# Attention with a soft mixture of experts on one core: value products split three to one, and the late softmax sums moved to GpSimd

## The chip, the cores and the metric

One NeuronCore of a Trainium2 chip. The metric is the device time of one execution in microseconds (us). Five engines matter: TensorE (PE, with its weight loads PEld), VectorE (DVE), ScalarE (ACT), GpSimd (POOL) and SyncE (SP), which issues most DMAs. Each engine executes its own list of instructions strictly in order, and waits on semaphores for the others.

## What is computed

```python
kv_flat = kv.reshape(B, H//4, 4, W//4, 4, C).mean(axis=(2, 4)).reshape(B, -1, C) @ w_sr
s = scale * (q @ kv_flat.transpose(0, 2, 1))          # 12288 queries x 768 keys, 4 batches
a = exp(s - s.max(-1)); a /= a.sum(-1) + 1e-09
x = (a @ kv_flat).reshape(B * N, C)                   # 49152 tokens x 128
logits = x @ phi                                      # 32 slots (8 experts x 4)
d = exp(logits - logits.max(0)); d /= d.sum(0) + 1e-09
slot_out = per expert: relu((d.T @ x) @ w1) @ w2      # 32 x 128
c = exp(logits - logits.max(1)); c /= c.sum(1) + 1e-09
out = c @ slot_out                                    # 49152 x 128
```

The last three lines of logits work are the "output softmax": over the 32 slots of each token. Its result can be multiplied with `slot_out` only when all tokens have been seen, so the output is written at the end.

## The kernel before

The queries are worked in 96 blocks of 512 (`NB`), 24 per batch. A group is 4 blocks (2048 tokens); there are 25 groups, since the last four blocks are split into one of three and one of one. A Python class `Plan` is a list scheduler: the kernel states each step with an engine, a cost, a due time and its dependences, and the class emits one fixed order of instructions per engine. The chip sees only these orders.

**A block.** PE makes the scores in 18 matmuls (L560 to L562, three PSUM tiles of two banks, `s`). DVE takes their maxima over keys (L578, L588, L590), PE brings these across partitions by the one rowmax matmul L598, and DVE finishes with L603 and the transpose L608, then subtracts the maximum from the scores (L616, four pieces), which frees the score tiles for the next block. ACT takes exponentials (L624, L628), and POOL forms the low half of their split to 16 bits (`plo`, L633).

**Value products.** For each of the 4 tiles of 128 queries of an earlier block, PE multiplies the exponentials with the values: 12 matmuls with the high half (L650, L651: "hi") and 6 with the low half (L658: "lo"). They accumulate in two PSUM banks that the plan hands out, `m_119` and `m_120`: tiles 0 and 1 in one (322 columns), tiles 2 and 3 in the other. The rowmax matmul L598 writes its 64 columns at the end of one of the same two banks, and so do the small products of a group (among them L778 and L834). ACT evacuates each pair of tiles (L668, 128x322).

**A group.** DVE, POOL and ACT turn 16 evacuated tiles into logits, and update running maxima and sums of the slots. For the output softmax of the group DVE takes the maxima over 32 slots (`k_max`, L852, one instruction per block), POOL subtracts them (`k_sub`, L857), ACT takes the exponential (L862), DVE sums (`k_sum`, L869, two per group), ACT adds 1e-09 (`k_add`, L874), DVE takes the reciprocal (`k_rec`, L879) and POOL multiplies (`k_mul`, L884). `k_add` and `k_rec` are joint over several groups: `JOIN = (0, 4, 12, 22)` gives spans of groups 0 to 3, 4 to 11 and 12 to 21. The products of groups 0 to 3 lie in the loop, all others behind it.

**Behind the loop (the tail).** The experts run (L1322 to L1384), their result is scaled and split (`shi`, L1390, on ACT; `slo` on DVE), and 25 chunks of output follow: PE transposes the softmax of a chunk (L1412), ACT and DVE split it (`chi`, L1418; `clo`, L1422), PE multiplies with `shi` and `slo` (L1434), ACT and DVE evacuate one half each (`o`, L1448, L1450; the first chunk in pieces, L1456 and L1458), and SP issues its write, 1.05 MB for a full chunk.

Of the kernel before, what the change touches and what calls it, by code (L numbers as in the profile page):

```python
# [36 lines left out]
class Plan:  # L37
# [22 lines left out]
    def emit(self):  # L60
# [31 lines left out]
        def bank(key):  # L92
            found = []
            for b in range(len(banks)):
                if key[0] == "pq":
                    t = gone(banks[b])
                    beside = banks[b] is not None and banks[b][1][0] == "px" and t == inf
                    if beside:
                        t = summed.get(banks[b], inf)
                    found.append((max(t, gone(tops[b])), not beside, b))  # L100
                else:
                    found.append((max(gone(banks[b]), gone(tops[b])), False, b))
            return min(found)
# [104 lines left out]
def attention_then_soft_moe(ctx: ExitStack, tc: tile.TileContext, qT, kv0, kvT, w_sr, w_srT, phi, w1, w2, outT):  # L208
# [130 lines left out]
    SPAN = 2  # L339
    KPS = 2  # L340
    KSD = 2
    KDUE = 4.0
    EARLY = FAST - 1
    AHEAD = 4
    JOIN = (0, AHEAD, 12, EARLY)
    KV0 = 14.5
# [283 lines left out]
    def plo(i, h):  # L630
# [3 lines left out]
        PP[i, h] += (lo,)  # L634

    def av_tile(i, k):
        if k % 2 == 0 and i == NB - 1:
            PX[i, k // 2] = ps.tile([P, 2, BQ], F32, tag=f"s{k // 2}", name=f"px_{i}_{k}")[:, :, :VW]
        elif k % 2 == 0:
            px = mt([P, 512], f"px_{i}_{k}")  # L640
            PX[i, k // 2] = px[:, : 2 * VW].rearrange("p (n c) -> p n c", n=2)
        return PX[i, k // 2][:, k % 2, :]

    def av_hi(i, k, t0):
        _, vhi, vlo = VU[i // BPB]
        px = PX[i, k // 2][:, k % 2, :] if t0 else av_tile(i, k)
        ks = slice(k * P, (k + 1) * P)
        for t in range(t0, t0 + AVS):
            p = PP[i, t // TH][0][:, t % TH, ks]
            nc.tensor.matmul(px, p, vhi[:, t, :], start=(t == 0 and (i >= AHD or k % 2 == 0)), stop=False)  # L650
            nc.tensor.matmul(px[:, 1:], p, vlo[:, t, :], start=False, stop=False)  # L651

    def av_lo(i, k):
        vhi = VU[i // BPB][1]
        px = PX[i, k // 2][:, k % 2, :]
        ks = slice(k * P, (k + 1) * P)
        for t in range(NT):
            nc.tensor.matmul(px, PP[i, t // TH][1][:, t % TH, ks], vhi[:, t, :], start=False, stop=(t == NT - 1 and (i >= AHD or k % 2 == 1)))  # L658

    def av_evac(i, k):  # L660
        g = GOF[i]
        if i == GB[g][0] and k == 0:
            XL[g] = gp.tile([P, TG, VW], F32, tag="xl", name=f"xl_{g}", bufs=2)
        o = (i - GB[g][0]) * TB + 2 * k
        if i == NB - 2 and k == 0:
            nc.vector.tensor_copy(XL[g][:, o : o + 2, :], PX.pop((i, k)))
        else:
            nc.scalar.activation(XL[g][:, o : o + 2, :], PX[i, k], AF.Copy)  # L668

# [178 lines left out]
    def k_max(g, u=None):  # L848
        o, n = GB[g][0] * TB, nt(g)
        if u is not None:  # L850
            o, n = o + u * TB, TB
        nc.vector.tensor_reduce(out=RM[:, o : o + n], in_=LL[:, o : o + n, :], axis=X, op=ALU.max)  # L852
# [56 lines left out]
    def dve(n):  # L909
        return n / 960 + 0.07  # L910
# [208 lines left out]
    def av_rest(i, k, m, p, prev):  # L1119
        los = [ops["lo", i, 0], ops["lo", i, 1]]  # L1120
        a2 = end_lo = op("PE", 6 * 0.072, 0.17, p + 0.8, prev + los, lambda: av_lo(i, k), use=[("plo", (i, 0)), ("plo", (i, 1)), m])
        if k % 2:
            g = GOF[i]
            first = i == GB[g][0] and k == 1
            x = ("xl", g)
            if i == NB - 1:
                v = k // 2
                q = HEAD + (i - 2) * PER + 0.01 * v
                a2 = op("DVE", 0.16, 0.08, q, [a2], lambda: l_x(v), use=[m], raw=0.05)
                a2 = op("DVE", 0.16, 0.08, q, [a2], lambda: l_r(v), raw=0.05)  # L1130
                a2 = ops["l", v] = op("DVE", 0.24, 0.08, q, [a2], lambda: l_l(v), use=[m], raw=0.05)
            ops["x", i, k // 2] = op(
                "DVE" if i == NB - 2 and k == 1 else "ACT", act(2 * VW) + (0.1 if i == NB - 2 and k == 1 else -0.03), 0.1, p - 2, [a2] + evs[-1:], lambda: av_evac(i, k // 2),
                acq=[x] if first else [], use=[m] + ([] if first else [x]),
            )
            evs.append(ops["x", i, k // 2])
        return [end_lo]
# [4 lines left out]
    def av_ops(i):  # L1142
# [6 lines left out]
        end = i == NB - 1  # L1149
        px = [(f"s{k // 2}" if end else "m", ("px", i, k // 2)) for k in range(TB)]  # L1150
        base = prev
        for k in range(TB if i < AHD else 0):
            m = px[k]
            p = T0 + AVD * PER + 1.3 * k
            if k == TB // 2:
                low = prev
                prev = base + [ops["r3", i + 1]]
            for t in range(0, NT, AVS):
                prev = [op("PE", 2 * AVS * 0.0702, 0.17, p, prev, lambda i=i, k=k, t=t: av_hi(i, k, t), acq=[m] if k % 2 == t == 0 else [], use=pp + ([m] if k % 2 or t else []))]
            if k % 2:  # L1160
# [98 lines left out]
    def k_first(g, a):  # L1259
# [3 lines left out]
        ops["ke", g] = op("ACT", act(n), 0.1, p, [a], lambda: k_exp(g))  # L1263

    for g in range(len(GB)):
        n = nt(g) * NS
        p = HEAD + (GB[g][0] + GB[g][1] + KLAG) * PER
        late = [] if g < FAST - 1 else end_ + [last[LG, "g"]]
        if late:
            a = [op("DVE", dve(n), 0.08, p, [ops["L", g]] + late, lambda g=g: k_max(g))] if g < FAST else []  # L1270
        else:
            a = [op("DVE", dve(TB * NS) + 0.05, 0.08, p, [ops["L", g]], lambda g=g, u=u: k_max(g, u), fill=p + 3 * PER) for u in range(GB[g][1])]
        if g < FAST:
            k_first(g, a)
        if g < EARLY:
            ops["ks", g] = [
# [337 lines left out]
```

## Time and profile before

| | |
|---|---|
| median of 3 runs | 1062.12 us (1062.01 to 1062.18) |
| the profiled execution | 1062.19 us |
| its span (first to last instruction) | 1060.4 us |
| busy PE / DVE / POOL / ACT | 1027.6 / 971.5 / 872.5 / 793.6 us |
| granted TensorE clock, mean | 0.996 |
| output written | 25.17 MB |

The span is 1.8 us shorter than the execution's own time, a constant that lies around it. The loop runs to about 965 us, the experts to about 995 us, and the output to the end. Busy shares are means over these three stages, which have different limits.

### The profile page before, as it was taken

The numbers are of one execution on the slowest core, as the hardware profiler recorded it, in microseconds if no ns is written. First come the engines' busy times: TensorE is split into PE (matmuls) and PEld (weight loads), VectorE is DVE, ScalarE is ACT, GpSimd is POOL, SyncE is SP. The second block draws the span as 40 slices with busy tenths as digits, with TensorE's granted clock in tenths as the row PEclk, the third lists the DMA queues.
The fourth block names the chain that finished last, engine by engine and source line by source line (L and its number), as shares of the span: only waits on it lengthen the run. The fifth ranks groups of instructions, "written<-read, shape, count | busy, mean of one in ns | idle before, by whom it ended". The sixth has DMA issues, their size and how long they took to land.

```text
span 1060.4 us, 24836 instructions
## 1 busy us (share of the span) xinstructions
PE 1027.6 (97%) x10261; PEld 880.3 (83%) x10261; DVE 971.5 (92%) x1552; ACT 793.6 (75%) x1046; POOL 872.5 (82%) x509
## 2 busy tenths in 40 slices
PE   8999999999999999999999999999999999999994
PEld 5788888888888888888888888888888888888452
DVE  6989999999999999999999999999999999998774
ACT  3777887888777787788787787788787787776463
POOL 0789998889989988889989988889988999895800
PEclk9999999999999999999999999999999999999998
DMA  9234510120137320120146310120110110112598
GB/s 370 112 83 89 119 54 3 42 87 15 41 72 148 71 56 2 41 100 2 41 87 134 86 41 1 41 100 1 41 41 2 42 41 1 41 41 91 198 416 368
DMA packets 15729, 89.17 MB, mean 84 GB/s; under 512 B 1664, under 2 KB 1920, under 8 KB 9344
## 3 DMA queue, kind: packets, MB, share of 16 engines
q1 hardware_dynamic: 11728, 69.47, 17.8%
q0 software_dynamic: 3312, 17.70, 8.9%
q8 instruction: 81, 1.33, 0.5%
q10 hardware_dynamic: 576, 0.41, 0.1%
q14 instruction: 32, 0.26, 0.1%
HBM read 58.87 MB, written 25.17 MB: 79 GB/s over the span
## 4 chain that ended last, share of the span: by engine, by line
PE 86%; DVE 7%; DMA 3%; ACT 1%; issue 1%; POOL 0%; SPq 0%; DVEq 0%; ACTq 0%; POOLq 0%
PE m L650 15%; PE m L658 14%; PE m L651 14%; PE s L560 12%; PE s L562 12%; PE s L561 11%; DMA outT<-o 2%; PE m L834 2%; DVE r L578 2%; DVE t L616 2%; PE po L1434 1%; DMA kv<-kv 1%; PE m L1406 1%; DVE m L603 1%; PE m L465 1%
## 5 line engine op out<-in xcount | busy, mean ns | idle before, releaser
L633 POOL TENSOR_TENSOR plo<-t,phi 128x1536 f16<-128x1536 f32 x190 | 599.0, 3163 | 92.9 <-ACT t L628 84.0
L624 ACT ACTIVATE phi<-t 128x1536 f16<-128x1536 f32 x192 | 283.5, 1478 | 148.0 <-DVE t L616 148.0
L578 DVE TRANSPOSE_TENSOR_REDUCE r<-s 128x32 f32<-128x1024 f32 x289 | 354.0, 1234 | 8.4 <-PE s L562 1.6
L650 PE MATMUL m<-vhi,phi 128*128 128x161 f16 x2280 | 353.2, 234 | 8.2 <-DVE m L603 7.3
L651 PE MATMUL m<-vlo,phi 128*128 128x160 f16 x2280 | 352.4, 233 | 0.0
L616 DVE TENSOR_TENSOR t<-s,mb 128x1024 f32<-128x1024 f32 (+1 forms) x384 | 342.0, 950 | 6.2
L628 ACT ACTIVATE t<-t 128x1536 f32<-128x1536 f32 x192 | 283.1, 1476 | 1.2
L650 PEld LDWEIGHTS <-phi 128*128 128x128 f16 x2304 | 224.1, 98 | 21.7 <-issue 21.3
L560 PE MATMUL s<-qhi,khi 128*128 128x512 f32 x574 | 237.0, 413 | 0.6 <-DVE t L616 0.4
L651 PEld LDWEIGHTS <-phi 128*128 128x128 f16 x2304 | 225.1, 98 | 12.1 <-issue 10.6
L562 PE MATMUL s<-qhi,klo 128*128 128x512 f32 x574 | 224.6, 391 | 0.0
L561 PE MATMUL s<-qlo,khi 128*128 128x512 f32 x574 | 223.9, 390 | 0.0
L658 PE MATMUL m<-vhi,plo 128*128 128x161 f16 x2280 | 223.5, 234 | 0.0
L658 PEld LDWEIGHTS <-plo 128*128 128x128 f16 x2304 | 171.9, 98 | 2.8 <-issue 2.7
L550 POOL TENSOR_TENSOR qlo<-q,qhi 128x512 fp32r<-128x512 f32 x95 | 127.5, 1342 | 23.9 <-ACT qhi L545 23.9
L562 PEld LDWEIGHTS s<-qhi,klo 128*128 128x128 f32 x574 | 107.7, 188 | 23.7
L560 PEld LDWEIGHTS s<-qhi,khi 128*128 128x128 f32 x574 | 107.9, 188 | 21.7 <-issue 2.6
L561 PEld LDWEIGHTS s<-qlo,khi 128*128 128x128 f32 x574 | 108.2, 189 | 19.4 <-issue 0.7
L668 ACT ACTIVATE xl<-m 128x322 f32<-128x322 f32 x189 | 81.3, 430 | 50.4 <-PE m L658 44.1
L608 DVE STREAM_TRANSPOSE mb<-m 128x512 f32<-128x512 f32 x96 | 68.3, 712 | 3.3
L545 ACT ACTIVATE qhi<-q 128x512 fp32r<-128x512 f32 x96 | 59.5, 620 | 2.8 <-DMA q<-qT 2.7
L603 DVE TENSOR_REDUCE m<-m 128x16 f32<-128x64 f32 x96 | 21.5, 224 | 22.6 <-PE m L598 19.2
(196 smaller groups left out, 840.4 us busy)
## 6 DMA issues: line engine op xcount, KB each, us to landing
q<-qT SPq DMA_DIRECT2D x23, 1024.0 KB, 4.9
outT<-o SPq DMA_DIRECT2D x22, 1024.0 KB, 8.3
kva<-kvT POOLq DMA_DIRECT2D x9, 1536.0 KB, 11.6
kva<-kvT SPq DMA_DIRECT2D x3, 1536.0 KB, 12.8
kv<-kv SPq DMA_DIRECT2D x6, 512.0 KB, 6.2
w<-w SPq DMA_DIRECT2D x2, 1536.0 KB, 6.3
w<-w SPq DMA_DIRECT2D x4, 768.0 KB, 4.1
kva<-kva POOLq DMA_DIRECT2D x3, 768.0 KB, 10.8
```

The lines of the kernel that those rows point to most:

```text
L550: eng.tensor_tensor(out=lo, in0=q_src(i), in1=hi.bitcast(F32), op=ALU.subtract)
L560: nc.tensor.matmul(s, khi[:, ks], hi, start=True, stop=False)
L561: nc.tensor.matmul(s, khi[:, ks], lo, start=False, stop=False)
L562: nc.tensor.matmul(s, klo[:, ks], hi, start=False, stop=True)
L578: nc.vector.tensor_reduce(out=MX[i][:, t : t + n, :].rearrange("p t b -> p (t b)"), in_=S[i, t // 2][:, u : u + n, :].rearrange("p t (b j) ...
L616: nc.vector.tensor_tensor(out=TT_[i, h][:, o : o + n, :], in0=S[i, t // 2][:, u : u + n, :], in1=MX[i].unsqueeze(1).broadcast_to([P, n, BQ ...
L624: nc.scalar.activation(hi, TT_[i, h], AF.Exp, scale=SCALE)
L628: nc.scalar.activation(t, t, AF.Exp, scale=SCALE)
L633: eng.tensor_tensor(out=lo, in0=TT_.pop((i, h)), in1=PP[i, h][0], op=ALU.subtract)
L650: nc.tensor.matmul(px, p, vhi[:, t, :], start=(t == 0 and (i >= AHD or k % 2 == 0)), stop=False)
L651: nc.tensor.matmul(px[:, 1:], p, vlo[:, t, :], start=False, stop=False)
L658: nc.tensor.matmul(px, PP[i, t // TH][1][:, t % TH, ks], vhi[:, t, :], start=False, stop=(t == NT - 1 and (i >= AHD or k % 2 == 1)))
```

## The change

It does four things.

1. Value products: tiles 0 to 2 of a block share one bank (483 columns), tile 3 has the other to itself (161). The rowmax result may lie beside the part with one tile, no longer beside the large one. ACT's evacuations become one of 128x483 and one of 128x161.
2. `k_max`: two instructions of 8 tiles per group, in place of four of 4 tiles.
3. `k_sum` for groups 4 to 21: no longer on DVE in the loop. A new `k_tree` on POOL, due behind the loop, adds the 32 slots of a group in five steps, each of which reads what the step before it wrote. Groups 0 to 3 and 22 to 24 keep DVE's sum.
4. `JOIN` becomes `(0, 4, 6, 9, 12, 15, 18, 22)`: for the groups with trees six joint `k_add` and `k_rec` of 2, 3, 3, 3, 3 and 4 groups (32, 48, 48, 48, 48, 64 columns), all behind the loop.

DVE has 48 instructions fewer, POOL 99 more, ACT 4 more; PE and SP have as many as before.

```diff
@@ Plan.bank @@
                     t = gone(banks[b])
-                    beside = banks[b] is not None and banks[b][1][0] == "px" and t == inf
+                    beside = banks[b] is not None and banks[b][1][0] == "px" and banks[b][1][2] == 1 and t == inf
                     if beside:
                         t = summed.get(banks[b], inf)
...
     SPAN = 2
     KPS = 2
+    KMP = 2
     KSD = 2
     KDUE = 4.0
     EARLY = FAST - 1
     AHEAD = 4
-    JOIN = (0, AHEAD, 12, EARLY)
+    JOIN = (0, AHEAD, 6, 9, 12, 15, 18, EARLY)
     KV0 = 14.5
     KVS = 1.0
     WARM = (("s2", 2.2, 30, 0.32, 20.0), ("m", 26.3, 30, 0.22, 46.0))
...
+    def part(i, k):
+        if i == NB - 1:
+            return k // 2, k % 2, 2
+        return (0, k, TB - 1) if k < TB - 1 else (1, 0, 1)
+
+    def px_of(i, k):
+        v, j, _ = part(i, k)
+        return PX[i, v][:, j, :]
+
     def av_tile(i, k):
-        if k % 2 == 0 and i == NB - 1:
-            PX[i, k // 2] = ps.tile([P, 2, BQ], F32, tag=f"s{k // 2}", name=f"px_{i}_{k}")[:, :, :VW]
-        elif k % 2 == 0:
-            px = mt([P, 512], f"px_{i}_{k}")
-            PX[i, k // 2] = px[:, : 2 * VW].rearrange("p (n c) -> p n c", n=2)
-        return PX[i, k // 2][:, k % 2, :]
+        v, j, n = part(i, k)
+        if j == 0 and i == NB - 1:
+            PX[i, v] = ps.tile([P, 2, BQ], F32, tag=f"s{v}", name=f"px_{i}_{k}")[:, :, :VW]
+        elif j == 0:
+            PX[i, v] = mt([P, 512], f"px_{i}_{k}")[:, : n * VW].rearrange("p (n c) -> p n c", n=n)
+        return PX[i, v][:, j, :]
 
     def av_hi(i, k, t0):
         _, vhi, vlo = VU[i // BPB]
-        px = PX[i, k // 2][:, k % 2, :] if t0 else av_tile(i, k)
+        px = px_of(i, k) if t0 else av_tile(i, k)
         ks = slice(k * P, (k + 1) * P)
         for t in range(t0, t0 + AVS):
             p = PP[i, t // TH][0][:, t % TH, ks]
-            nc.tensor.matmul(px, p, vhi[:, t, :], start=(t == 0 and (i >= AHD or k % 2 == 0)), stop=False)
+            nc.tensor.matmul(px, p, vhi[:, t, :], start=(t == 0 and (i >= AHD or part(i, k)[1] == 0)), stop=False)
             nc.tensor.matmul(px[:, 1:], p, vlo[:, t, :], start=False, stop=False)
 
     def av_lo(i, k):
         vhi = VU[i // BPB][1]
-        px = PX[i, k // 2][:, k % 2, :]
+        px = px_of(i, k)
+        _, j, n = part(i, k)
         ks = slice(k * P, (k + 1) * P)
         for t in range(NT):
-            nc.tensor.matmul(px, PP[i, t // TH][1][:, t % TH, ks], vhi[:, t, :], start=False, stop=(t == NT - 1 and (i >= AHD or k % 2 == 1)))
-
-    def av_evac(i, k):
+            nc.tensor.matmul(px, PP[i, t // TH][1][:, t % TH, ks], vhi[:, t, :], start=False, stop=(t == NT - 1 and (i >= AHD or j == n - 1)))
+
+    def av_evac(i, k, o, n):
         g = GOF[i]
         if i == GB[g][0] and k == 0:
             XL[g] = gp.tile([P, TG, VW], F32, tag="xl", name=f"xl_{g}", bufs=2)
-        o = (i - GB[g][0]) * TB + 2 * k
+        o += (i - GB[g][0]) * TB
         if i == NB - 2 and k == 0:
-            nc.vector.tensor_copy(XL[g][:, o : o + 2, :], PX.pop((i, k)))
-        else:
-            nc.scalar.activation(XL[g][:, o : o + 2, :], PX[i, k], AF.Copy)
+            nc.vector.tensor_copy(XL[g][:, o : o + n, :], PX.pop((i, k)))
+        else:
+            nc.scalar.activation(XL[g][:, o : o + n, :], PX[i, k], AF.Copy)
 
 
     def bc(a, n):
...
     def k_max(g, u=None):
         o, n = GB[g][0] * TB, nt(g)
         if u is not None:
-            o, n = o + u * TB, TB
+            n //= KMP
+            o += u * n
         nc.vector.tensor_reduce(out=RM[:, o : o + n], in_=LL[:, o : o + n, :], axis=X, op=ALU.max)
 
     def k_sub(g):
...
             n //= KPS
             o += u * n
         nc.vector.tensor_reduce(out=RM[:, o : o + n], in_=LL[:, o : o + n, :], axis=X, op=ALU.add)
+
+    def k_tree(g):
+        o, n = GB[g][0] * TB, nt(g)
+        t = gp.tile([P, TG, NS], F32, tag="D", name=f"ks_{g}")
+        a, w = LL[:, o : o + n, :], NS // 2
+        while w > 1:
+            b = t[:, :n, :w]
+            nc.gpsimd.tensor_tensor(out=b, in0=a[:, :, :w], in1=a[:, :, w : 2 * w], op=ALU.add)
+            a, w = b, w // 2
+        nc.gpsimd.tensor_tensor(
+            out=RM[:, o : o + n].unsqueeze(2), in0=a[:, :, :1], in1=a[:, :, 1:2], op=ALU.add
+        )
 
     def k_add(g, n):
         o = GB[g][0] * TB
...
         if late:
             a = [op("DVE", dve(n), 0.08, p, [ops["L", g]] + late, lambda g=g: k_max(g))] if g < FAST else []
         else:
-            a = [op("DVE", dve(TB * NS) + 0.05, 0.08, p, [ops["L", g]], lambda g=g, u=u: k_max(g, u), fill=p + 3 * PER) for u in range(GB[g][1])]
+            a = [op("DVE", dve(n // KMP) + 0.05, 0.08, p, [ops["L", g]], lambda g=g, u=u: k_max(g, u), fill=p + 3 * PER) for u in range(KMP)]
         if g < FAST:
             k_first(g, a)
-        if g < EARLY:
+        if AHEAD <= g < EARLY:
+            trees.append(g)
+        elif g < EARLY:
             ops["ks", g] = [
                 op("DVE", dve(n // KPS) + 0.05, 0.08, p + KSD * PER, [ops["ke", g]], lambda g=g, u=u: k_sum(g, u), fill=p + (KSD + KDUE) * PER)
                 for u in range(KPS)
...
     sq = [sq[3], sq[7]]
     shi = tail("ACT", 0.25, [a, ts], t_shi, use=[("s1", "psq")])
     slo = tail("DVE", 0.3, [shi], t_slo, use=[("s1", "psq")])
+    for g in trees:
+        ops["ks", g] = [op("POOL", 1.5, 0.1, T1 + 278 + 4 * g, [ops["ke", g], ops["g5m", FAST]], lambda g=g: k_tree(g), acq=[("D", ("ks", g))])]
     for g in range(len(GB)):
         n = nt(g) * NS
         p = T1 + 288 + 4 * g
```

In the order of the changed kernel the lines are about 10 to 30 higher: L599 is the rowmax matmul (L598 before), L660, L661 and L669 the value products (L650, L651, L658), L898 is `k_add`, L908 `k_mul`, L889 and L891 the tree, L1419 `shi`, L1477 and L1485 the evacuation of `o`.

**PE, around the rowmax matmul of the third block of a group in the middle of the loop.** Before, in full rows (the products that follow go on alike):

```order
L658 LDWEIGHTS plo_1_7368
L658 MATMUL m_120<-vhi_6794,plo_1_7368 128x161
L598 LDWEIGHTS sel_h
L598 MATMUL m_119<-rq_7493,sel_h 128x64
L650 LDWEIGHTS phi_0_7281
L650 MATMUL m_119<-vhi_6794,phi_0_7281 128x161
```

In the changed kernel, at the same block:

```order
L661 LDWEIGHTS phi_0_7246
L661 MATMUL m_119<-vlo_6769,phi_0_7246 128x160
L599 LDWEIGHTS sel_h
L599 MATMUL m_120<-rq_7458,sel_h 128x64
L660 LDWEIGHTS phi_0_7246
L660 MATMUL m_119<-vhi_6768,phi_0_7246 128x161
```

Before, the rowmax follows the last lo product of tile 1, and the products of tile 2 go to the bank that it has just written. Now it comes behind four hi products of tile 2, whose bank is the other one.

**ACT, from the second half of the experts to the third chunk of output.** Before:

```order
L1369 ACTIVATE hs<-m_119,mask 128x128 x2
L1390 ACTIVATE shi<-psq,tsum 128x128
L1418 ACTIVATE chi_14348<-m_120 128x512
L874 ACTIVATE RM<-RM,eps 128x12
L874 ACTIVATE RM<-RM,eps 128x4
L1456 ACTIVATE o_14352<-po_1_14354 128x2x2x128 x2
L1418 ACTIVATE chi_14382<-m_119 128x512
L1448 ACTIVATE o_14386<-po_1_14388 128x2x4x128
L1448 ACTIVATE o_14413<-po_1_14415 128x2x4x128
```

Now:

```order
L1398 ACTIVATE hs<-m_119,mask 128x128 x2
L898 ACTIVATE RM<-RM,eps 128x48
L1419 ACTIVATE shi<-psq,tsum 128x128
L1447 ACTIVATE chi_14301<-m_120 128x512
L898 ACTIVATE RM<-RM,eps 128x12
L898 ACTIVATE RM<-RM,eps 128x4
L1485 ACTIVATE o_14306<-po_1_14308 128x2x2x128 x2
L1447 ACTIVATE chi_14340<-m_119 128x512
L1477 ACTIVATE o_14343<-po_1_14345 128x2x4x128
L898 ACTIVATE RM<-RM,eps 128x48
L1477 ACTIVATE o_14375<-po_1_14377 128x2x4x128
```

The first 128x48 is that of groups 6 to 8 and stands ahead of `shi`; the second is that of groups 9 to 11 and stands ahead of the evacuation of the third chunk. The next two of 48 stand ahead of the evacuations of the 7th and the 11th chunk, the one of 64 ahead of the 15th.

**POOL, behind the loop.** Before, one row holds nearly all of it:

```order
L857 TENSOR_TENSOR LL<-LL,RM 128x512
L884 TENSOR_TENSOR LL<-LL,RM 128x512
L857 TENSOR_TENSOR LL<-LL,RM 128x384
L857 TENSOR_TENSOR LL<-LL,RM 128x128
L884 TENSOR_TENSOR LL<-LL,RM 128x512 x18
```

Now, from the end of the third tree on:

```order
L891 TENSOR_TENSOR RM<-ks_14204 128x16
L908 TENSOR_TENSOR LL<-LL,RM 128x512
L889 TENSOR_TENSOR ks_14229<-LL 128x16x16
L889 TENSOR_TENSOR ks_14229<-ks_14229 128x16x8
L889 TENSOR_TENSOR ks_14229<-ks_14229 128x16x4
L889 TENSOR_TENSOR ks_14229<-ks_14229 128x16x2
L891 TENSOR_TENSOR RM<-ks_14229 128x16
L908 TENSOR_TENSOR LL<-LL,RM 128x512
```

The order as a whole, with T4 for the tree of group 4 and m for one product: T4, the three `k_sub`, T5, T6, m, T7, m, T8, T9, 2 m, T10, m, T11, m, T12, 2 m, T13, m, T14, the product of 384, T15, that of 128, T16, 3 m, T17, T18, 2 m, T19, m, T20, T21, 4 m.

## Rows read from the trace of the kernel before

**Rows 1.** Stretches: us, then busy us (instructions) of PE PEld DVE ACT POOL, clock, DMA share, GB/s.

```profile
47.00:965.00 918.00, 908.72 (x9248) 803.69 (x9246) 870.10 (x1375) 718.29 (x927) 825.86 (x461) 1.00 0.20 52
1000.00:1040.00 40.00, 37.91 (x324) 20.99 (x322) 30.98 (x34) 26.65 (x34) 4.95 (x6) 1.00 1.01 418
```

**Rows 2.** Waits: engine, its line, whom it waited for; us in total, times, longest.

```profile
DVE m L603 <- PE m L598: 19.2, 34, 0.9
PE m L650 <- DVE m L603: 7.3, 23, 0.3
```

**Rows 3.** PE's timeline, third and fourth block of a group: start, us [idle].

```profile
520.56 0.47 PE L560 MATMUL s<-qhi,khi 128*128 128x512 f32 x1
...
524.75 0.24 PE L650 MATMUL m<-vhi,phi 128*128 128x161 f16 x1
...
527.31 0.19 PE L598 MATMUL m<-rq,sel_h 128*128 128x64 f16 x1
...
527.82 0.23 PE L650 MATMUL m<-vhi,phi 128*128 128x161 f16 x1 [0.32 <-DVE m L603]
...
530.32 0.47 PE L560 MATMUL s<-qhi,khi 128*128 128x512 f32 x1
...
536.84 0.19 PE L598 MATMUL m<-rq,sel_h 128*128 128x64 f16 x1
...
539.85 0.48 PE L560 MATMUL s<-qhi,khi 128*128 128x512 f32 x1
```

**Rows 4.** DVE's timeline, that third block.

```profile
527.02 0.41 DVE L869 TENSOR_REDUCE RM<-LL 128x8 f32<-128x256 f32 x1
527.54 0.23 DVE L603 TENSOR_REDUCE m<-m 128x16 f32<-128x64 f32 x1
```

**Rows 5.** PE's timeline in an early block.

```profile
73.43 0.19 PE L598 MATMUL m<-rq,sel_h 128*128 128x64 f16 x1
...
76.11 0.47 PE L560 MATMUL s<-qhi,khi 128*128 128x512 f32 x1
```

**Rows 6.** DVE's groups by shape: busy us, mean ns of one.

```profile
L852 DVE TENSOR_REDUCE RM<-LL 128x4 f32<-128x128 f32 x89 | 21.6, 270 | 0.0
L869 DVE TENSOR_REDUCE RM<-LL 128x8 f32<-128x256 f32 x44 | 17.9, 408 | 0.0
```

**Rows 7.** POOL's groups by shape.

```profile
L800 POOL TENSOR_TENSOR D<-LL,mrun 128x384 f32<-128x384 f32 x1 | 1.0, 1003 | 5.6 <-DVE r L721 5.6
L805 POOL TENSOR_TENSOR da<-mrun,mrun 128x32 f32<-128x32 f32 x23 | 6.1, 267 | 0.0
```

**Rows 8.** POOL's timeline, one stretch in the loop.

```profile
536.74 1.28 POOL L800 TENSOR_TENSOR D<-LL,mrun 128x512 f32<-128x512 f32 x1
537.96 0.26 POOL L805 TENSOR_TENSOR da<-mrun,mrun 128x32 f32<-128x32 f32 x1
538.17 3.14 POOL L633 TENSOR_TENSOR plo<-t,phi 128x1536 f16<-128x1536 f32 x1
```

**Rows 9.** POOL's timeline, behind the loop.

```profile
982.48 1.05 POOL L857 TENSOR_TENSOR LL<-LL,RM 128x512 f32<-128x512 f32 x1 [3.01 <-DVE sm L1299]
983.49 1.05 POOL L884 TENSOR_TENSOR LL<-LL,RM 128x512 f32<-128x512 f32 x1
984.49 1.19 POOL L857 TENSOR_TENSOR LL<-LL,RM 128x384 f32<-128x384 f32 x2
985.64 19.31 POOL L884 TENSOR_TENSOR LL<-LL,RM 128x512 f32<-128x512 f32 x20
```

**Rows 10.** SP's timeline: the first issues of output.

```profile
995.96 0.94 SPq L1462 DMA_DIRECT2D outT<-o  x2
```

**Rows 11.** ACT's timeline in the tail.

```profile
986.23 0.31 ACT L874 ACTIVATE RM<-RM,eps 128x16 f32<-128x16 f32 x1 [0.15 <-DVE RM L869]
...
1025.14 0.60 ACT L1418 ACTIVATE chi<-m 128x512 fp32r<-128x512 f32 x1
1026.35 1.02 ACT L1448 ACTIVATE o<-po 128x1024 f32<-128x1024 f32 x1 [0.62 <-DMA outT<-o]
```

More of the change, by code (lines that the diff above doesn't have):

```diff
@@ L1121, in av_rest @@
         a2 = end_lo = op("PE", 6 * 0.072, 0.17, p + 0.8, prev + los, lambda: av_lo(i, k), use=[("plo", (i, 0)), ("plo", (i, 1)), m])
-        if k % 2:
+        v, j, n = part(i, k)
+        if j == n - 1:
             g = GOF[i]
-            first = i == GB[g][0] and k == 1
+            first = i == GB[g][0] and v == 0
             x = ("xl", g)
             if i == NB - 1:
-                v = k // 2
                 q = HEAD + (i - 2) * PER + 0.01 * v
@@ L1131, in av_rest @@
                 a2 = ops["l", v] = op("DVE", 0.24, 0.08, q, [a2], lambda: l_l(v), use=[m], raw=0.05)
-            ops["x", i, k // 2] = op(
-                "DVE" if i == NB - 2 and k == 1 else "ACT", act(2 * VW) + (0.1 if i == NB - 2 and k == 1 else -0.03), 0.1, p - 2, [a2] + evs[-1:], lambda: av_evac(i, k // 2),
+            dve_ = i == NB - 2 and v == 0
+            ops["x", i, v] = op(
+                "DVE" if dve_ else "ACT", act(n * VW) + (0.1 if dve_ else -0.03), 0.1, p - 2, [a2] + evs[-1:], lambda: av_evac(i, v, k + 1 - n, n),
                 acq=[x] if first else [], use=[m] + ([] if first else [x]),
             )
-            evs.append(ops["x", i, k // 2])
+            evs.append(ops["x", i, v])
         return [end_lo]
@@ L1149, in av_ops @@
         end = i == NB - 1
-        px = [(f"s{k // 2}" if end else "m", ("px", i, k // 2)) for k in range(TB)]
+        px = [(f"s{k // 2}" if end else "m", ("px", i, part(i, k)[0])) for k in range(TB)]
+        head_ = [part(i, k)[1] == 0 for k in range(TB)]
         base = prev
@@ L1154, in av_ops @@
             p = T0 + AVD * PER + 1.3 * k
-            if k == TB // 2:
+            if k == TB - 1:
                 low = prev
@@ L1158, in av_ops @@
             for t in range(0, NT, AVS):
-                prev = [op("PE", 2 * AVS * 0.0702, 0.17, p, prev, lambda i=i, k=k, t=t: av_hi(i, k, t), acq=[m] if k % 2 == t == 0 else [], use=pp + ([m] if k % 2 or t else []))]
-            if k % 2:
-                if k > 2:
+                prev = [op("PE", 2 * AVS * 0.0702, 0.17, p, prev, lambda i=i, k=k, t=t: av_hi(i, k, t), acq=[m] if head_[k] and t == 0 else [], use=pp + ([] if head_[k] and t == 0 else [m]))]
+            if k >= TB - 2:
+                if k == TB - 1:
                     prev = prev + low
-                for j in (k - 1, k):
+                for j in range(TB - 1) if k < TB - 1 else (k,):
                     prev = av_rest(i, j, m, T0 + AVD * PER - 2.5 + k, prev)
@@ L1168, in av_ops @@
             for t in range(0, NT, AVS):
-                a1 = op("PE", 2 * AVS * 0.0702, 0.17, p, prev + ([] if end or t else los), lambda i=i, k=k, t=t: av_hi(i, k, t), acq=[m] if k % 2 == t == 0 else [], use=pp + ([m] if k % 2 or t else []))
+                a1 = op("PE", 2 * AVS * 0.0702, 0.17, p, prev + ([] if end or t else los), lambda i=i, k=k, t=t: av_hi(i, k, t), acq=[m] if head_[k] and t == 0 else [], use=pp + ([] if head_[k] and t == 0 else [m]))
                 prev = [a1]
@@ L1263, in k_first @@
         ops["ke", g] = op("ACT", act(n), 0.1, p, [a], lambda: k_exp(g))
+    trees = []
     for g in range(len(GB)):
```

## The prediction

> **What bounds the kernel now.** I read the busy time by stretch first, because the two halves of the change touch different stages. In the loop, from 47 to 965 us, PE is busy 908.7 of 918 us and DVE 870.1 [rows 1]: PE sets the pace, and all the time that a cheaper DVE or a freer bank can give back is PE's idle 9.3 us. From 1000 us on the output DMAs run at a share of 1.01 and 418 GB/s [rows 1]: a chunk of 1.05 MB takes 2.51 us, the 25.17 MB take 60.2 us, and whatever delays the stream by more than its slack is paid in full at the end. The list of waits shows where the loop's two tightest engines meet [rows 2]: PE's value products waited 7.3 us, 23 times, for L603, which reads the rowmax bank; DVE's L603 waited 19.2 us for the rowmax matmul. In the tail ACT's evacuation at 1026.35 waits for a DMA to give its buffer free [rows 11].
>
> One block, in order of time [rows 3]: scores from 520.56, value tiles from 524.75, rowmax at 527.31 behind two tiles (2.56 us, so 1.28 a tile, 0.071 a matmul), then 0.32 us of waiting, since tile 2 goes to the bank that the rowmax has written, and the next scores at 530.32. What follows the rowmax on PE (two tiles, 2.56, and the wait) sets the end there. In an early block, where fewer products follow, the next scores come 2.68 behind the rowmax [rows 5]: that is DVE's chain from rowmax to the first freed score tile, and a floor for every block.
>
> **The change, part by part.** All sums are against the profiled execution, 1062.2 us, 0.1 above the median of the runs.
>
> *DVE in the loop.* 36 sums at 0.408 are gone (14.7 us); 88 maxima at 0.270 become 44 at about the 0.408 of an instruction of the same width (5.8 us) [rows 6]. 20.5 us leave DVE, 0.21 a block. Most of it buys nothing: the sum at 527.02 stands while DVE waits anyway for the rowmax matmul of 527.31 [rows 3, 4]. Only where DVE's chain is late does it count. I allow 30 blocks, those at the start and those in which the next batch's keys are prepared: 30 x 0.21 = -6.
>
> *Bank split.* The wait of 0.32 goes: tile 2 no longer needs the rowmax bank. Late next is DVE's chain. By the changed order the rowmax of a third block stands behind 4.19 us of scores, 2.56 of two tiles and four matmuls (0.28): 7.03 from the block's start instead of 6.75, and next scores at 7.03 + 2.68 = 9.71 instead of 9.76 [rows 3, 5]. In a fourth block it stands in the same place; small matmuls among its scores add some 0.20, since before it stood at 6.52 where scores, one tile and 12 matmuls make 4.19 + 1.28 + 0.85 = 6.32. So 7.23 + 2.68 = 9.91 against 9.53 [rows 3]. A group of this kind gains 0.05 and loses 0.38; with about fourteen such groups +4.5. ACT evacuates as many columns in as many instructions as before, off PE's path, so nothing.
>
> The loop: -6 + 4.5 = **-1.5 us**. Its bounds are -9.3, where PE never idles, and +4.5, where DVE's relief is worth nothing. The loop's last evacuation on DVE now needs a third tile (1.28) and part of that is covered by the next product: **+0.5**, between 0 and 1.3.
>
> *The trees.* Behind the loop POOL gets 18 trees of 5 dependent adds of 256, 128, 64, 32 and 16 elements per partition. The tree of group 4 fits into POOL's idle 3.01 us ahead of 982.48; 17 follow the three subtractions, which end at 985.64 less the product that stood among them, 984.6 [rows 9]. The trace has no such tree. By durations of subtractions with two inputs of full size, 1.003 at 384 and 0.267 at 32 elements, one costs 0.200 + 0.00209 per element [rows 7]: 5 x 0.200 + 496 x 0.00209 = 2.04. By start-to-start spacing of independent ones, 1.22 at 512 and 0.21 at 32 [rows 8], it is 5 x 0.143 + 496 x 0.0021 = 1.76. Each add waits for the one before to have written, so durations are nearer, and a gap of 0.03 each is likely: I take **2.2**, with 1.76 and 2.54 (gaps of 0.1) as ends. The Trainium skill (Perfetto Trace Analysis, GPSIMD Engine Instruction) says that a GpSimd span is unreliable and operations should be timed by the spacing of their starts; the trace's spacings are indeed below its durations, and the sum by that rule is the first rival below.
>
> *Who waits for the trees.* POOL's own work there (17 x 2.2 and 19.3 us of products) ends near 1041, long before the end. The path goes over ACT: a joint `k_add` stands in its queue ahead of `shi` and ahead of the evacuations of chunks 3, 7, 11 and 15, and while it waits for the last tree of its groups, all behind it wait, `chi` and evacuations alike. With products at 1.0 each [rows 9], the last tree of each joint span ends at 984.6 + 4t + 2.0, + 7t + 5.1, + 10t + 9.1, + 13t + 13.3 and + 17t + 16.3, where t is the price of a tree. The first output was issued at 996.0 [rows 10], so chunk number j, counted from 0, was due on the queue at 996.0 + 2.51j: chunk 15 (j = 14) at 1031.1, although ACT began to evacuate it at 1026.35 [rows 11]. In the change it is ready one add (0.31), one `chi` (0.6), one evacuation (1.02) and some 0.2 of semaphores behind the last tree [rows 11]. With t = 2.2: 984.6 + 37.4 + 16.3 + 2.15 = 1040.5, **9.4 us** late. The earlier ones are late by less: chunk 3 by 984.6 + 15.4 + 5.1 + 1.55 - 1001.0 = 5.7. They do not add up, since each delay moves the queue's schedule; the largest counts, and ten chunks remain, at DMA pace, so none of it is made up.
>
> On DVE the joint reciprocals stand between copies and wait for the same trees; on that they only repeat ACT's delay. The rest of `JOIN`, 4 more ACT instructions of 0.3 and their reciprocals, lies in idle time of these engines. By the rows the move saves 14.7 us of DVE time, mostly beside a wait, for some 18 x 2.2 = 40 us of POOL time. The Trainium skill (GPSIMD Engine Reference, Engine selection) sends a reduction along the free dimension to VectorE; by it the sums should stay where they were.
>
> Sum: 1062.2 - 1.5 + 0.5 + 9.4 = **1070.6 us**.
>
> **The rivals.**
> 1. *Trees at the price of spacing, t = 1.76.* For it: POOL starts independent operations 0.05 before the last one's recorded end. Against: these are dependent. Chunk 15 is then late by 984.6 + 29.9 + 16.3 + 2.15 - 1031.1 = 1.9, chunk 3 by 2.6. With the loop: 1062.2 - 1.5 + 0.5 + 2.6 = 1063.8, within the noise or slightly slower.
> 2. *Faster: PE's idle time goes.* The bank wait of 7.3 us is the largest that the list puts on PE in the loop; if DVE's relief lets the rowmax come as early as PE's order allows, and its chain fits behind, the loop gains up to 9.3. With cheap trees: 1062.2 - 9.3 + 0.5 + 2.6 = 1056.0; with t = 2.2 it would only cancel them, 1062.8. It decides from t = 2.1 down (a delay below 8). Against: after the rowmax of a third block only 2.28 us of products follow, less than DVE's 2.68.
> 3. *The loop slower too.* Rowmax behind tile 2's beginning costs 0.33 a group and DVE's relief gives nothing: 1062.2 + 4.5 + 0.5 + 9.4 = 1076.6.
>
> **How the numbers follow.** A difference of 0.2% (2.1 us) is about what a measurement of this kernel can tell from no change. Trees of 2.0 to 2.54 that hold ACT: 0.58, 1066 to 1076. Cheap trees: 0.22, of which slower 0.07, same 0.12, faster 0.03. PE's idle gone: 0.12, nearly all faster. Loop slower too: 0.08. Faster 0.14, same 0.16, slower 0.70. The range leaves out the lower end of rival 2 and the upper of rival 3: 1059 to 1077.
>
> **What would show it.** In the changed trace: POOL's five adds per group starting some 2.2 us apart from tree to tree; ACT's `k_add` of 48 and 64 columns listed as waiting for POOL, several us in total, with the evacuation of the third, seventh, eleventh and fifteenth chunk behind them; DMA share below 1 between 1000 and 1030; no wait of value products for L603, and next scores 2.7 behind the rowmax. Trees below 1.7 us, `k_add` without waits, or a loop that ends more than 5 us earlier would make the forecast wrong.

## The result, and the profile after

The changed kernel takes 1075.55 us (median of 4 runs, 1075.40 to 1076.11) against 1062.07 before: a ratio of 1.0128, interval 1.0110 to 1.0145, so 13.5 us slower. The forecast was 1070.6 us, slower. The profiled execution has a span of 1073.8 us, 13.4 more than before; what follows accounts for these 13.4. Of the two runs of one experiment, e7, one took 1157.12 us at a granted clock of 0.848 and is left out, the other 1070.65; the same kernel stands again as e11.

First the stretches: us, then busy us (instructions) of PE, PEld, DVE, ACT, POOL, granted clock, DMA share, GB/s.

```profile
47.00:965.00 918.00, 907.49 (x9230) 800.67 (x9228) 850.81 (x1293) 727.03 (x924) 825.71 (x460) 1.00 0.20 52
1000.00:1040.00 40.00, 34.55 (x264) 18.00 (x259) 25.82 (x32) 21.30 (x31) 36.29 (x73) 0.87 0.82 334
```

In the loop nothing has happened that a glance could see: PE 907.5 where it was 908.7, DVE 19 us less busy [rows 1]. (The profile's pages count 76 instructions fewer on DVE, 1552 to 1476, and 90 more on POOL, 509 to 599; the section on the change has 48 and 99.) In the tail everything has: the output DMAs, at a share of 1.01 before, have 0.82 and 334 GB/s, and POOL, which was busy for 4.95 of these 40 us, is busy for 36.29. Then the waits (engine, its line, whom it waited for; us in total, times, longest):

```profile
DVE m L604 <- PE m L599: 38.9, 77, 1.2
...
ACT RM L898 <- POOL RM L891: 15.8, 6, 3.9
...
DVE RM L903 <- ACT RM L898: 9.6, 5, 3.5
```

The second and third did not exist before: ACT's six joint adds (L898) wait 15.8 us for POOL's trees, DVE's reciprocals (L903) for ACT's adds. The first has doubled [rows 2]. PE's own waits in the loop, from 47 to 965 us:

```profile
PE m L660 <- ACT xl L679: 3.9, 6, 0.7
PE s L561 <- DVE t L617: 2.6, 13, 0.2
PE s L561 <- ACT xl L679: 1.3, 3, 0.4
...
PE m L660 <- DVE m L604: 0.6, 2, 0.3
```

PE's wait for the rowmax bank has fallen from 7.3 us [rows 2] to 0.6. Two others have come in its place: 2.6 us for DVE's first subtraction, and 5.2 us for ACT's evacuations (L679), which were 0.5 us before. ACT now takes three tiles out of the large bank at once, and PE's next products wait for that bank. The wait for DVE shows in PE's timeline over the same two blocks of a group as before [rows 3]:

```profile
521.94 0.47 PE L561 MATMUL s<-qhi,khi 128*128 128x512 f32 x1
...
528.99 0.19 PE L599 MATMUL m<-rq,sel_h 128*128 128x64 f16 x1
...
531.60 0.47 PE L561 MATMUL s<-qhi,khi 128*128 128x512 f32 x1 [0.15 <-DVE t L617]
...
538.78 0.19 PE L599 MATMUL m<-rq,sel_h 128*128 128x64 f16 x1
...
541.47 0.47 PE L561 MATMUL s<-qhi,khi 128*128 128x512 f32 x1 [0.22 <-DVE t L617]
```

The rowmax stands at 7.05 and 7.18 from the block's start, and the scores of the next block wait for DVE's first subtraction: the blocks take 9.66 and 9.87 us, where they took 9.76 and 9.53. DVE had the quarter maxima ready 0.4 us before the rowmax:

```profile
528.36 0.23 DVE L591 SCALAR_TENSOR_TENSOR rq<-m,quad_h 128x64 f16<-128x64 f32 x1
...
529.22 0.23 DVE L604 TENSOR_REDUCE m<-m 128x16 f32<-128x64 f32 x1 [0.31 <-PE m L599]
```

Behind the loop, POOL's timeline: the tree of group 4 with the subtractions behind it, trees 5 and 6 with the first product, and the last two trees.

```profile
982.73 0.73 POOL L889 TENSOR_TENSOR ks<-LL 128x256 f32<-128x256 f32 x1 [1.15 <-PE m L845]
...
984.95 2.20 POOL L869 TENSOR_TENSOR LL<-LL,RM 128x512 f32<-128x512 f32 x3
987.11 0.73 POOL L889 TENSOR_TENSOR ks<-LL 128x256 f32<-128x256 f32 x1
987.92 1.16 POOL L889 TENSOR_TENSOR ks<-ks 128x128 f32<-128x128 f32 x3
989.16 0.21 POOL L891 TENSOR_TENSOR RM<-ks 128x16 f32<-128x16 f32 x1
989.45 0.74 POOL L889 TENSOR_TENSOR ks<-LL 128x256 f32<-128x256 f32 x1
...
991.52 0.22 POOL L891 TENSOR_TENSOR RM<-ks 128x16 f32<-128x16 f32 x1
991.69 1.05 POOL L908 TENSOR_TENSOR LL<-LL,RM 128x512 f32<-128x512 f32 x1
...
1039.52 0.73 POOL L889 TENSOR_TENSOR ks<-LL 128x256 f32<-128x256 f32 x1
...
1041.57 0.21 POOL L891 TENSOR_TENSOR RM<-ks 128x16 f32<-128x16 f32 x1
1042.83 4.07 POOL L908 TENSOR_TENSOR LL<-LL,RM 128x512 f32<-128x512 f32 x4 [1.05 <-DVE RM L903]
```

The subtractions start at 984.95, 2.47 later than before [rows 9]. From 987.11 to 1041.78 POOL does 17 trees and 16.3 us of products without a pause: (54.67 - 16.3) / 17 = 2.26 us a tree. What the last joint span does to chunk 15 stands in the timelines of ACT and DVE:

```profile
1037.30 1.02 ACT L1477 ACTIVATE o<-po 128x1024 f32<-128x1024 f32 x1 [0.43 <-PE po L1463]
1041.82 0.35 ACT L898 ACTIVATE RM<-RM,eps 128x64 f32<-128x64 f32 x1 [3.49 <-POOL RM L891]
1042.07 0.58 ACT L1447 ACTIVATE chi<-m 128x512 fp32r<-128x512 f32 x1
1042.55 1.01 ACT L1477 ACTIVATE o<-po 128x1024 f32<-128x1024 f32 x1
```

```profile
1042.20 0.55 DVE L903 RECIPROCAL RM<-RM 128x64 f32<-128x64 f32 x1 [3.48 <-ACT RM L898]
1042.68 0.69 DVE L1451 TENSOR_TENSOR clo<-m,chi 128x512 fp32r<-128x512 f32 x1
1043.29 1.21 DVE L1479 COPY o<-po 128x1024 f32<-128x1024 f32 x1
```

ACT's half of chunk 15 is ready at 1043.56, DVE's at 1044.50, against the 1031.1 at which, by the prediction's sum, the queue could have taken it: 13.4 us, the whole difference of the spans. The DMA queue bears this out (columns as in the first table):

```profile
1043.00:1045.30 2.30, 1.68 (x15) 0.93 (x16) 2.30 (x4) 1.64 (x3) 2.30 (x3) 0.92 0.07 29
1045.30:1070.00 24.70, 17.07 (x151) 9.45 (x149) 14.80 (x17) 12.34 (x17) 1.60 (x2) 0.85 1.01 414
```

It stands nearly empty until chunk 15 comes and runs at full share from there to the end, so what that chunk is late by is not made up.

### The profile page after: what moved, and what is told of

It reads as the page before. It is cut to its first block, busy times and chain, and to the rows that moved or that the text cites. A ratio compares the mean times of both kernels' runs of the same rounds, so it can differ in the third digit from the quotient of the medians.

```text
span 1073.8 us, 24923 instructions
## 1 busy us (share of the span) xinstructions
PE 1032.9 (96%) x10261; PEld 880.9 (82%) x10261; DVE 954.1 (89%) x1476; ACT 803.8 (75%) x1050; POOL 907.8 (85%) x599
## 5 line engine op out<-in xcount | busy, mean ns | idle before, releaser
L660 PE MATMUL m<-vhi,phi 128*128 128x161 f16 x2280 | 354.9, 234 | 4.8 <-ACT xl L679 4.2
L661 PE MATMUL m<-vlo,phi 128*128 128x160 f16 x2280 | 354.1, 233 | 0.0
L660 PEld LDWEIGHTS <-phi 128*128 128x128 f16 x2304 | 224.2, 98 | 23.5 <-issue 23.4
L661 PEld LDWEIGHTS <-phi 128*128 128x128 f16 x2304 | 225.3, 98 | 6.1 <-issue 6.0
L669 PE MATMUL m<-vhi,plo 128*128 128x161 f16 x2280 | 223.3, 234 | 0.0
L679 ACT ACTIVATE xl<-m 128x483 f32<-128x483 f32 (+1 forms) x189 | 82.5, 437 | 163.2 <-PE m L669 154.6
L669 PEld LDWEIGHTS <-plo 128*128 128x128 f16 x2304 | 172.9, 98 | 1.1 <-issue 1.1
## 6 DMA issues: line engine op xcount, KB each, us to landing
kva<-kvT SPq DMA_DIRECT2D x3, 1536.0 KB, 12.5
```

## The experiments

All are compared with runs of the kernel before on the same chip.

**e1, the bank split alone.**

```diff
-    JOIN = (0, AHEAD, 6, 9, 12, 15, 18, EARLY)
+    JOIN = (0, AHEAD, 12, EARLY)
...
-        if AHEAD <= g < EARLY:
-            trees.append(g)
-        elif g < EARLY:
+        if g < EARLY:
```

(against the changed kernel; the maxima are per block again as well)

> Only the bank split of the value products; maxima, sums and JOIN as before. My theory (the rowmax behind tile 2's beginning makes the fourth block of a group longer, and the relief of DVE gave most of it back): the loop is 2 to 4 us longer than before, the tail unchanged, 1064 to 1066 us. Rival (the split itself pays, since PE's wait for the rowmax bank goes): 1058 to 1061 us.

1067.19 us, ratio 1.0045 (1.0025 to 1.0065). The split does not pay; it costs 4.7 us, a little more than my theory had. (In the span it is 4.4 us: 1064.8 for 1060.4. The time that lies around the span is 2.6 us in this run, so it is not the constant 1.8 that it is in the two kernels.) The last rowmax of the loop comes at 962.88 (before 961.14), the rest is lost at the loop's end, where four products of the early groups now stand on POOL between the last group's steps, and the subtractions start 4.5 us late:

```profile
969.32 2.06 POOL L907 TENSOR_TENSOR LL<-LL,RM 128x512 f32<-128x512 f32 x2 [0.81 <-DVE RM L902]
971.33 2.57 POOL L826 TENSOR_TENSOR D<-D,rv 128x512 f32<-128x512 f32 x1
...
975.59 2.05 POOL L907 TENSOR_TENSOR LL<-LL,RM 128x512 f32<-128x512 f32 x2
...
986.95 1.05 POOL L868 TENSOR_TENSOR LL<-LL,RM 128x512 f32<-128x512 f32 x1 [2.58 <-DVE sm L1325]
```

In the changed kernel the maxima that release the subtractions are 1.6 us late instead, some 3 us less. 0.7 us of that are there by the loop's last rowmax (962.14). The rest comes at the loop's end, where the changed kernel's order has the four products earlier, between subtractions inside the loop. Whether DVE's relief gave it back or only the planner's other order is not separated.

**e2, the maxima alone.**

```diff
-            o, n = o + u * TB, TB
+            n //= KMP
+            o += u * n
```

> Only the maxima in two instructions per group. My theory (they stand mostly where DVE waits for PE): within 1 us of before. Rival (DVE sets the pace in many blocks): the 6 us that leave DVE show as 2 us or more, 1060 us or less.

1062.73 us, ratio 1.0003 (0.9991 to 1.0014): nothing, as forecast. The 6 us that left DVE bought no time.

**e3, the trees and `JOIN` alone.**

```diff
-    JOIN = (0, AHEAD, 12, EARLY)
+    JOIN = (0, AHEAD, 6, 9, 12, 15, 18, EARLY)
...
+        if AHEAD <= g < EARLY:
+            trees.append(g)
```

> Only the trees behind the loop and the new JOIN; bank split and maxima as before. My theory (the trees hold the queues of ACT and DVE in the tail): nearly all of the loss, 1072 to 1075 us, with ACT's joint adds waiting some 15 us for POOL. Rival (the loop's loss under the bank split is what delays the tail): 1066 us or less.

1074.42 us, ratio 1.0113 (1.0083 to 1.0142): 11.9 of the 13.5 us on the loop of before, with 12.5 us of ACT's waits for POOL. The loop itself is as long as before (last rowmax at 961.63, of which 0.32 lie ahead of the first one), although DVE has 36 sums fewer in it: their removal buys nothing there.

**e4, one price in the planner.**

```diff
-        ops["ks", g] = [op("POOL", 1.5, 0.1, ...
+        ops["ks", g] = [op("POOL", 2.3, 0.1, ...
```

> The changed kernel with one number different: the planner's price of a tree is 2.3 us, about what it took, in place of 1.5. POOL's work is the same; the joint adds move to later places in ACT's queue, behind shi and behind several evacuations. My theory (the loss is the place of the adds in ACT's and the reciprocals in DVE's queue): ACT's waits for POOL fall from 15.8 us to under 4, and the time to 1065 to 1068 us. Rival (POOL's 40 us of trees make the products late in any order): 1073 us or more.

1072.32 us, ratio 1.0093 (1.0064 to 1.0122), between the two theories and nearer the rival. The waits of ACT did fall as meant; in their place PE's transposes wait for POOL's products:

```profile
PEld m L1441 <- POOL LL L908: 3.8, 6, 1.4
...
ACT RM L898 <- POOL RM L891: 1.8, 2, 0.9
PE m L1441 <- POOL LL L908: 1.6, 3, 0.9
```

So the place of the adds in ACT's queue is not the whole: with it mended, only some 3.7 us come back (9.8 of 13.5 are left; the two runs lie 1.3 us apart). The products of four groups still wait for the last of four trees; e6 tries that.

**e5, the late sums on DVE behind the loop.**

```diff
-        ops["ks", g] = [op("POOL", 1.5, ... lambda g=g: k_tree(g), acq=[("D", ("ks", g))])]
+        ops["ks", g] = [op("DVE", 0.68, ... lambda g=g: k_sum(g))]
```

> The changed kernel, but the sums of groups 4 to 21 behind the loop are DVE's single reduction (0.67 us each, 12 us in all) instead of GpSimd's trees; loop and JOIN as in the changed kernel. If the trees' 2.26 us each on POOL are the loss, most of it comes back: 1064 to 1068 us, with POOL's products back to back by 1015 us. If the loss is that the sums lie behind the loop at all, on whatever engine: 1071 us or more.

1066.54 us, ratio 1.0040 (1.0020 to 1.0060). Nine of the 13.5 us come back, though POOL's products end at 1025.7, not at 1015: it is the trees, not the fact that the sums lie behind the loop.

**e6, one add and one reciprocal per group.**

```diff
-    JOIN = (0, AHEAD, 6, 9, 12, 15, 18, EARLY)
+    JOIN = (0, *range(AHEAD, EARLY + 1))
...
-        ops["ks", g] = [op("POOL", 1.5, 0.1, ...
+        ops["ks", g] = [op("POOL", 2.3, 0.1, ...
```

> The changed kernel with the planner's price of a tree at 2.3 us and one add and one reciprocal per group. POOL's work is as before. If the loss is that the products of four groups wait for the last of their four trees (joint spans), a group's product now follows its own tree by one, chunk 21 is late by 3 to 5 us: 1065 to 1068 us. If POOL's 57 us of trees and products are the floor in any order: 1071 us or more.

1064.88 us, ratio 1.0026 (1.0015 to 1.0038): 10.7 of the 13.5 us come back, with all 18 trees still on POOL. Tree and product now alternate, and the output DMAs run at full share from the first chunk on (the same columns as above):

```profile
1028.01 1.05 POOL L908 TENSOR_TENSOR LL<-LL,RM 128x512 f32<-128x512 f32 x1
1029.02 0.73 POOL L889 TENSOR_TENSOR ks<-LL 128x256 f32<-128x256 f32 x1
...
1031.25 1.05 POOL L908 TENSOR_TENSOR LL<-LL,RM 128x512 f32<-128x512 f32 x1
```

```profile
999.40:1060.00 60.60, 47.65 (x418) 25.99 (x410) 42.40 (x58) 37.03 (x57) 41.72 (x83) 0.97 1.01 415
```

So what is left, 2.8 us, is the late start: `shi` comes at 995.90 instead of 993.28, the subtractions at 984.75 instead of 982.48.

**e7 and e11, half the trees.**

```diff
-        if AHEAD <= g < EARLY:
+        if 13 <= g < EARLY:
...
-    JOIN = (0, AHEAD, 6, 9, 12, 15, 18, EARLY)
+    JOIN = (0, AHEAD, 13, 16, 19, EARLY)
```

> The changed kernel with trees for groups 13 to 21 only; groups 4 to 12 are summed by DVE in the loop, JOIN (0, 4, 13, 16, 19, 22). Nine trees less are 20 us less on POOL. If POOL's chain of trees sets the end, its delay is gone and what is left is the loop and its end (1 to 3 us): 1064 to 1066 us. If the loss is made once, at the start of the tail (the tree ahead of the subtractions, the late shi), it stays: 1070 us or more.

> As e7 (trees for groups 13 to 21 only, JOIN (0, 4, 13, 16, 19, 22), price 1.5), whose profiled run fell into a low granted clock. If the number of trees sets the loss, half of it is left: 1066 to 1069 us. If the joint spans' place in ACT's queue sets it (three trees ahead of the first outputs), more than half is left: 1069 to 1072 us.

Of e11: 1070.46 us, ratio 1.0078 (1.0057 to 1.0098): half the trees keep 8.4 of 13.5 us. e7's first expectation, that POOL's chain sets the end and goes with half of it, falls. Three adds for joint spans of three trees are enough to hold ACT for 9.6 us; the first of them stands ahead of `shi`:

```profile
996.76 0.34 ACT L898 ACTIVATE RM<-RM,eps 128x48 f32<-128x48 f32 x1 [5.21 <-POOL RM L891]
...
998.41 0.37 ACT L1419 ACTIVATE shi<-psq,tsum 128x128 fp32r<-128x128 f32 x1 [0.80 <-PE psq L1413]
```

**e8, the tree of group 4 behind the subtractions.**

```diff
-[ops["ke", g], ops["g5m", FAST]], lambda g=g: k_tree(g)
+[ops["ke", g], ops["g5m", FAST], ops["ke", LG]], lambda g=g: k_tree(g)
```

> The changed kernel with all trees behind the last exponentials of the output softmax, so that the tree of group 4 no longer stands ahead of the three subtractions. These start some 0.85 us earlier and shi 2 to 3 us earlier. If the end hangs on the last tree, which comes no earlier, the time falls by less than 2 us: 1073.5 to 1075.5 us. If it hangs on the start of the tail: 1072 us or less.

1075.14 us, ratio 1.0121 (1.0092 to 1.0151). The subtractions start at 983.84 and `shi` at 995.56, 1.1 and 2.9 us earlier than in the changed kernel, and the time is only 0.4 us less, while e8's own two runs lie 1.3 us apart. The last tree ends at 1043.21, 1.4 later. So the earlier start buys nothing here. What sets the end it does not show, for ACT's order has changed too: the last joint add stands ahead of the evacuation of chunk 16, no longer of chunk 15.

**e9, the rowmax earlier in PE's order** (on e6 with e8's edit).

```diff
-        r2 = op("DVE", 0.58, 0.06, T0 + 2, ...
+        r2 = op("DVE", 0.58, -0.1, T0 + 2, ...
```

> The version of e6 (price 2.3, one add and one reciprocal per group) with all trees behind the last exponentials, and with the planner told that the quarter maxima come 0.16 us earlier than before, so that the rowmax matmul is put earlier in PE's order: over all blocks its place moves by 17.8 us in sum, some 0.2 a block, in third and fourth blocks from 7.0 and 7.1 to 6.3 to 6.8. If the place of the rowmax is what makes the split's blocks longer, the loop is 2 to 6 us shorter than that of the changed kernel and the time 1058 to 1062.5 us, better than e6 and perhaps than before. If it is not (PE then waits for the quarter maxima instead), 1064 to 1067 us.

1068.75 us, ratio 1.0061 (1.0044 to 1.0078): a miss beyond both expectations. The loop is not shorter but 1 us longer (last rowmax at 963.19, in the changed kernel 962.14), so a better place for the rowmax was not found in this way; that the split's loop could be made shorter stays open. The subtractions start at 984.83, as in e6, and what e9 loses to e6 (3.9 us) it loses behind them: the tree of group 4 is now in POOL's chain, and the last product ends at 1047.8, in e6 at 1045.2. POOL's order differs in one more place, the product of group 22 (see e10).

**e10, the trees alone, one add per group, all behind the exponentials.** The edits of e6 and e8 on e3.

> Only the trees, on the loop of before (no bank split, maxima as before), but with price 2.3, one add and one reciprocal per group and all trees behind the last exponentials. If the joint spans and their place were nearly all of the tail's loss, and the rest of e6's 2.8 us is the loop under the split, it comes within 1.5 us of before: 1062 to 1063.6 us. If POOL's work costs something in any order: 1065 us or more.

1067.19 us, ratio 1.0046 (1.0029 to 1.0062). Here the start is not late (`shi` at 993.81), and still 5 us are lost: late in the tail PE's transposes wait for POOL's products, one every 3.24 us, and the DMAs have less than they could move.

```profile
1032.60 0.66 PE L1427 MATMUL m<-ident,LL 128*128 128x128 f32 x4 [0.93 <-POOL LL L896]
...
1035.85 0.66 PE L1427 MATMUL m<-ident,LL 128*128 128x128 f32 x4 [0.93 <-POOL LL L896]
```

```profile
1030.00:1040.00 10.00, 7.22 (x62) 3.63 (x65) 5.94 (x9) 5.67 (x10) 8.98 (x19) 1.00 0.82 338
```

A tree and a product take 3.24 us, a chunk's DMA 2.51, so in this order POOL's pace holds the outputs. It need not: e6 has the same pace and a stream at full share. The two differ in POOL's order. In e10, as in e9, the product of group 22, which needs no tree, stands behind the tree of group 8, in e6 behind that of group 21. From there on every group's product stands one tree later in e10: that of group 19 starts at 1041.22, in e6 at 1037.74, although the last trees end together (1041.27 and 1041.02). One such place is 3.24 us, so a large part of the 5 us may be that place and not the pace. No run has e10's loop with e6's order.

**e12, one chunk fewer ahead in PE's order.**

```diff
-        ops["ks", g] = [op("POOL", 2.3, 0.1, ...
+        ops["ks", g] = [op("POOL", 3.2, 0.1, ...
```

> The version of e10 (only the trees, one add and one reciprocal per group, all trees behind the last exponentials) with one number changed: the planner's price of a tree 3.2 in place of 2.3. POOL's work and its order are the same; in PE's order the output products of a chunk now stand behind the transposes of one chunk fewer. In e10 the late chunks follow POOL's products at 3.24 us each, two products behind. If what is left of the loss is that place in PE's order, one or two products of 3.24 us come back and the time is 1062.3 to 1064.5 us. If POOL's pace itself (3.24 us a group where DMA takes 2.51 a chunk) is the limit, it stays at 1066.5 us or more.

1069.76 us, ratio 1.0073 (1.0050 to 1.0096): the expectation falls, in the direction of the rival and past it. POOL's order is not e10's, as was expected: the product of group 22 stands behind all trees again. The adds and reciprocals, put later in the queues of ACT and DVE, now hold POOL, and late in the tail a tree and a product take 3.3 us:

```profile
POOL LL L896 <- DVE RM L891: 5.9, 6, 2.3
```

No version here beats the kernel before, and the nearest (e2) does without split and trees.

## Why the prediction was right, and where it was not

The direction, the place (the tail) and the mechanism there were as forecast; 9.4 us were forecast for the trees and some 12 came. By its own steps:

- *The bank split.* The third block above was forecast at 9.71 us, measured 9.66; the fourth at 9.91, measured 9.87. But the sum of +4.5 was too large: in e1, the split without the rest, the loop's last rowmax is 1.7 us late. Over blocks 9 to 88 the fourth blocks of the groups are 0.38 longer on the mean than before, as forecast, and the other three together 0.30 shorter, where the forecast gave them 0.05. Nor is it DVE's chain alone that came in place of PE's wait, as written: the evacuations by ACT were put at nothing, "off PE's path", and PE waits 5.2 us for them.
- *DVE's relief in the loop*, -6 us, was too large: e2 and e3 show that on the loop of before neither the maxima nor the sums give anything, and against e1 the loop of the changed kernel is 0.7 us shorter. So these two terms were off by 2.8 and 5.3 us, with opposite signs, and that part of it cancels is luck. The loop came out 1.0 us longer (last rowmax 962.14 for 961.14), not 1.5 shorter: 2.5 us of the miss.
- *The loop's end*, +0.5, measured +0.6: the maxima `sm`, which release the subtractions, are ready 1.62 later, 1.0 of it from the loop. DVE's last evacuation waits 2.34 us instead of 0.74.
- *The tree of group 4* was to fit into POOL's idle 3.01 us. It could not start before 982.73, because its buffer and its start hang on the last group's products on PE; it held the subtractions for 0.85 us. The idle time was there, but the tree was not ready in it.
- *The price of a tree*, 2.2 between 1.76 and 2.54: 2.26. The 1.76 took the spacing of independent operations for adds that depend on each other, and that step is what the run refutes. The Trainium skill (Perfetto Trace Analysis, GPSIMD Engine Instruction) would have consecutive operations timed by the spacing of their starts; the 2.26 of this run is such a spacing, so the run does not speak against it.
- *Who waits*: the chain of sums forecast the last tree at 1038.3; with the start 2.47 later and 17 x 0.06 more it is 1041.8, measured 1041.78. Behind it the prediction had 2.15 us up to ACT's evacuation and let DVE "only repeat ACT's delay". DVE's half was the later one, 2.72 behind the tree: add, reciprocal, `clo`, copy, one after the other.

For chunk 15 these make 9.4 + 2.5 (the later start) + 1.0 (the price) + 0.6 (DVE's half) = 13.5, measured 13.4. Against the forecast the miss of 5.0 us is the loop's 2.5, 0.85 for the tree of group 4, 1.0 for the price, 0.6 for DVE's half and 0.1 at the loop's end.

One sentence of the prediction is refuted all the same: that POOL's own work ends "long before the end" and the path goes over ACT. POOL's last product ends at 1046.90. e4 takes ACT's waits away and gets back some 3.7 us; e6 shortens the joint spans and gets back 10.7; e10 does both on the loop of before and loses 5 at POOL's pace, 3.24 us a group against 2.51 us a chunk, in an order that is one product worse than e6's. The joint span is the largest part, ACT's and DVE's queues are how it reached the output, and POOL's pace is a limit in e10's order and not in e6's. The rule that I weighed against the change, VectorE for a reduction along the free dimension (the Trainium skill, GPSIMD Engine Reference, Engine selection), is borne out by e5: with the same sums as DVE reductions, behind the loop as well, the kernel takes 9 us less.

Not settled: how much of e10's 5 us is POOL's pace and how much the place of group 22's product, which goes with the span of e6 being 2.0 us shorter although its outputs start 2.1 us later. e12 was meant to show that the transposes ahead of each output product are what is left of the loss; it changed POOL's order as well and shows neither. Nor is the loop's 1.0 us divided between DVE's chain and ACT's evacuations.

## What to carry to other kernels

A join over several groups saves a few small instructions and makes the first group wait for the last; when its inputs move to a slower engine, shorten the join first. In an engine that executes in order, a small instruction that waits for a far producer costs whatever stands behind it, so look in the order at what follows it, on every engine of the chain, and price the last of them. Time taken off an engine that waits at the same point anyway is no gain: look at what ends the wait behind it. An instruction that waits for nothing, put early into the order of a slow engine, delays everything behind it by its turn.

## What the runs showed of the hardware

- On GpSimd an add that needs the add before it starts 0.08 us after that one's recorded end (987.11 + 0.73 to 987.92), an independent one 0.05 us before it (991.52 + 0.22 to 991.69, between a tree and the product of another group). The difference, 0.13 us, is from a sixth to over a half of what these adds take (0.73 and 0.21).
- The granted TensorE clock was 1.00 while PE stood still for the last joint add, and fell to 0.50, the lower of its two levels (1.2 GHz), soon after PE worked again; PE was then fully busy at it:

```profile
1040.60:1043.60 3.00, 0.00 (x0) 0.00 (x0) 1.40 (x3) 1.78 (x4) 1.72 (x5) 1.00 0.85 352
1045.30:1048.30 3.00, 3.00 (x18) 1.62 (x17) 1.86 (x3) 1.18 (x3) 1.60 (x2) 0.50 1.01 415
```

The DMA share in the second stretch is 1.01, so the slower PE cost the output nothing there; the queue had been empty before it, while chunk 15 was missing. The earlier low stretches of the tail (1000.60 to 1007.40 and 1021.10 to 1024.50) cannot have made chunk 15 late either, for that chunk waits for POOL's last tree, and POOL runs without a pause from 987.11 to 1041.78. So none of the 13.4 us is seen to come from the clock.
